# Projection of the queries in one step of 512 tokens and a short one, weight conversion without GpSimd, and a new order of all steps

## The chip, the cores and the metric

The kernel runs on one core of one Trainium2 chip. The metric is the device time of one launch in microseconds (us); three runs of the kernel before the change gave 1080.97, 1083.51 and 1084.04 us, with a median of 1083.51 us. One further execution was taken with the profiler: 1081.44 us, of which 1079.7 us lie between its first and its last instruction (the span). Five queues work side by side on the core: PE (TensorE, the matmuls), DVE (VectorE), ACT (ScalarE), POOL (GpSimd), and SP (SyncE), which here only issues DMAs. Each runs its own instructions strictly in the order in which they were written.

## What is computed

The reference is a linear attention with positive features, followed by a feed-forward layer whose activation is h cos(h). There are 8 batches of 8 heads, 576 tokens, a head size of 64, 128 features, a model width of 512 and a hidden width of 2048:

```python
def phi(x):
    proj = np.einsum('bhsd,df->bhsf', x, w_phi)
    proj = proj - np.max(np.abs(proj), axis=-1, keepdims=True)
    return np.concatenate([np.exp(proj), np.exp(-proj)], axis=-1)
q_p, k_p = (phi(q), phi(k))
kv = np.einsum('bhsf,bhsd->bhfd', k_p, v)
z = np.sum(k_p, axis=2)
num = np.einsum('bhsf,bhfd->bhsd', q_p, kv)
den = np.einsum('bhsf,bhf->bhs', q_p, z)[..., None] + 1e-06
attn = num / den                       # [8, 8, 576, 64]
x = attn.transpose(0, 2, 1, 3).reshape(4608, 512)
h = x @ w_in                           # [4608, 2048]
out = (h * np.cos(h)) @ w_out          # [4608, 512]
```

## The kernel before

**Units and visits.** Two heads form a pair, called a unit; there are 32 units (`attention(u)`). A unit's queries and keys lie with the 64 rows of one head on partitions 0 to 63 and those of the other on 64 to 127. The feed-forward layer works on chunks of 512 tokens; a `visit` takes one chunk through some or all of the 16 blocks of the hidden width. Each block needs one weight tile (a slice of both weight matrices).

**Feed-forward matmuls.** They are split in three products of a fast 32-bit format (high times high, high times low, low times high): `mm1` is 12 matmuls of 512 columns (line 782), `mm2` another 12 (lines 816 to 818). There are 144 of each in all.

**Weight tiles.** `convert(ft)` makes the high and low parts of a tile from the 64-bit inputs. ACT scales (lines 350, 351), DVE does three bit operations on 1024 columns (lines 355 to 359), ACT makes the high part, and three more elementwise instructions follow, `rest` (line 366), `low` (recorded as line 54) and `add` (line 372). `W_POOL` names the tiles for which POOL does these last three; it holds tiles 0 to 3. DVE does them for the other twelve. The first two visits need tiles 0 to 3, the third also 4 to 7, so these are converted while the first units run.

**Queries of a unit.** `q_mm(hf)` projects 288 tokens of both heads, one matmul for each head on its own half of the rows (line 434); it is called twice, as two steps. ACT copies the four results out of PSUM (`q_copy`, line 441), DVE reduces each to a maximum over blocks of 32 (`q_red`, line 445), then folds the maxima (lines 453, 454). POOL copies 32 partitions to the other three quarters (`q_spread`, line 459), DVE turns the maxima back into columns (`q_turn`, line 463), and POOL subtracts them from the projections (`q_sub`, line 467, two of 576 columns). ACT takes the exponentials (line 587).

**Keys of a unit.** `k_mm` projects 512 tokens of each head (line 476, eight small matmuls on half of the rows each) and `k_end` the last 64 of both heads in one full matmul (line 552). DVE takes the maxima (line 564). For the first eight units PE subtracts them in PSUM (`k_sub`, line 574), for the others DVE does (line 569).

**Shapes on PE.** Four shapes of the array are in use: all 128 x 128 (mm1, mm2, k_end, k_sub), rows in two halves (q_mm, k_mm), columns in two halves (lines 626, 632 and 675), and columns in four quarters (line 665). The 64-row pairs, the column pairs and the column quarters run side by side.

**What sets the order.** Every piece of work is a `Step` with an engine and an estimated cost. The table `ORDER` lists the numbers of all steps, 2920 of them, and the kernel issues them in that order; nothing is decided on the chip. A step's place in its engine's queue, and its PSUM bank, follow from the table. The steps touched by the change are those of `attention` for the queries and those of `convert` for tiles 0 to 3.

Of the kernel before, what the change touches and what calls it, by code (L numbers as in the profile page):

```python
# [17 lines left out]
P = 128  # L18
TWO_PI = 6.283185307179586
PI_2 = 1.5707963267948966  # L20
CT = 512
# [4 lines left out]
def phi_attention_then_cos_ffn(ctx: ExitStack, tc: tile.TileContext, qT, kT, vS, vT, w_phi, w_in, w_out, out):  # L26
# [41 lines left out]
    class Step:  # L68
# [16 lines left out]
    SHAPE = dict(mm1="full", mm2="full", one="full", k_mm="upper", k_end="full", t_mm="upper", t_end="full", s_mm="full", k_sub="full", kv_mm="left", n_mm="left", z_mm="quarter", q_mm="upper")  # L85
    ORDER = [
# [189 lines left out]
    def bank(b):  # L276
        return banks[b.slot]
# [26 lines left out]

    GROUP = 3
    Q_DVE = range(0)
    Q_SUMS = range(0)  # L310
    K_SUMS = range(8)
    WARM = 7
    WHOLE = 8
    W_POOL = range(4)
    Q = NFT // 4
    quarter = [list(range(Q * i, Q * i + Q)) for i in range(4)]
# [616 lines left out]
```

## Time and profile before

| what | value |
|---|---|
| median of three runs | 1083.51 us |
| the profiled execution, its own time | 1081.44 us |
| its span | 1079.7 us |
| mean granted TensorE clock | 1.000 |
| busy in the span: PE, ACT, DVE, POOL | 1069.3, 720.8, 711.8, 157.6 us |
| moved by DMA | 160.72 MB |

Busy time adds up every moment in which at least one instruction of an engine ran. For PE it says little by itself: matmuls overlap and their ends are modelled, so the interval from one start to the next is what counts. The prediction therefore reads PE's cost from starts in the timeline, and the cost of DVE, ACT and POOL from durations.

### The profile page before, as it was taken

The page shows a single profiled execution, that of the slowest core. Times are in us where ns is not written, and L with a number is a line of the kernel's source. Part 1 is how long each engine was busy: PE and PEld are TensorE (multiplying, and loading weights), DVE is VectorE, ACT ScalarE, POOL GpSimd, SP SyncE. Part 2 cuts the span into 40 slices and gives each one's busy share as a digit, 9 for nine tenths or more (in the row PEclk, how much of TensorE's full clock was granted, in tenths as well). Part 3 has the DMA queues.
Part 4 walks back from the last instruction along what each step waited for, and adds up shares of the span by engine and source line. Part 5 has one row for each costly group of instructions (what it writes and reads, how often), then busy time and mean ns, then how long its engine had stood idle before and what let it go on. Part 6 is the DMA issues. An engine that isn't in the chain of part 4 may idle for free.

```text
span 1079.7 us, 19604 instructions
## 1 busy us (share of the span) xinstructions
PE 1069.3 (99%) x7678; PEld 830.6 (77%) x7678; DVE 711.8 (66%) x1203; ACT 720.8 (67%) x1388; POOL 157.6 (15%) x187
## 2 busy tenths in 40 slices
PE   9999999999999999999999999999999999999998
PEld 6666677787888887788677787786877878888886
DVE  6899999988898877645667456764564353434333
ACT  7888898878666669754785766757556654544443
POOL 5664322000000310101121011120120000000000
PEclk9999999999999999999999999999999999999999
DMA  7535644667655544275242643163231720540541
GB/s 217 154 119 189 180 132 143 209 202 249 235 167 191 210 153 153 105 242 185 63 123 73 243 148 107 56 232 135 75 87 47 277 90 1 187 174 10 185 157 49
DMA packets 92604, 160.72 MB, mean 149 GB/s; under 512 B 43744, under 2 KB 52064, under 8 KB 84320
## 3 DMA queue, kind: packets, MB, share of 16 engines
q1 hardware_dynamic: 92352, 159.41, 44.3%
q8 instruction: 60, 0.98, 0.4%
q14 instruction: 32, 0.26, 0.1%
q10 hardware_dynamic: 160, 0.07, 0.0%
HBM read 117.51 MB, written 41.94 MB: 148 GB/s over the span
## 4 chain that ended last, share of the span: by engine, by line
PE 87%; DVE 5%; issue 0%; DMA 0%; POOL 0%; ACT 0%; DVEq 0%; POOLq 0%
PE bank L782 36%; PE bank L816 12%; PE bank L818 12%; PE bank L817 12%; PE bank L675 4%; PE bank L626 4%; PE bank L665 2%; PE bank L434 2%; PE bank L476 2%; PE bank L632 1%; PE bank L552 1%; DMA out<-o_last 0%; DVE g_c__1300 L793 0%; DVE g_c__1130 L800 0%; DVE m_u__1584 L445 0%
## 5 line engine op out<-in xcount | busy, mean ns | idle before, releaser
L797 ACT ACT_TABLE_LOAD x23 | 29.5, 1283 | 0.4
L459 POOL COPY m_u__4056<-m_u__4056 32x36 f32<-32x36 f32 x3 | 1.6, 540 | 174.4 <-DVE m_u__4056 L454 174.3
L582 ACT ACT_TABLE_LOAD x15 | 19.2, 1283 | 0.8 <-DVE pk_u__2466 L569 0.5
L856 DVE TENSOR_TENSOR o<-bank,o 128x512 f32<-128x512 f32 x24 | 16.1, 678 | 0.1
L863 ACT ACTIVATE o<-bank 128x512 f32<-128x512 f32 x16 | 9.5, 592 | 5.5 <-PE bank L818 5.5
L782 PE MATMUL bank<-xh_c__6319,w 128*128 128x512 f32 x32 | 12.9, 402 | 0.0
L865 DVE COPY o<-bank 128x512 f32<-128x512 f32 x16 | 10.8, 674 | 3.1 <-PE bank L818 3.1
L782 PE MATMUL bank<-xh_c__5560,w 128*128 128x512 f32 x32 | 12.7, 398 | 0.0
L782 PE MATMUL bank<-xh_c__7588,w 128*128 128x512 f32 x32 | 12.7, 396 | 0.0
L782 PE MATMUL bank<-xh_c__4428,w 128*128 128x512 f32 x32 | 12.6, 393 | 0.0
L782 PE MATMUL bank<-xh_c__6921,w 128*128 128x512 f32 x32 | 12.5, 391 | 0.0
L782 PE MATMUL bank<-xh_c__6769,w 128*128 128x512 f32 x32 | 12.5, 390 | 0.0
L782 PE MATMUL bank<-xh_c__5807,w 128*128 128x512 f32 x32 | 12.5, 390 | 0.0
L782 PE MATMUL bank<-xh_c__7130,w 128*128 128x512 f32 x32 | 12.5, 390 | 0.0
L782 PE MATMUL bank<-xh_c__5878,w 128*128 128x512 f32 x32 | 12.5, 390 | 0.0
L782 PE MATMUL bank<-xh_c__7977,w 128*128 128x512 f32 x32 | 12.5, 390 | 0.0
L782 PE MATMUL bank<-xh_c__5928,w 128*128 128x512 f32 x32 | 12.5, 390 | 0.0
L782 PE MATMUL bank<-xh_c__8059,w 128*128 128x512 f32 x32 | 12.5, 390 | 0.0
L782 PE MATMUL bank<-xh_c__4632,w 128*128 128x512 f32 x32 | 12.5, 389 | 0.0
L782 PE MATMUL bank<-xh_c__8100,w 128*128 128x512 f32 x32 | 12.5, 389 | 0.0
L782 PE MATMUL bank<-xh_c__4557,w 128*128 128x512 f32 x32 | 12.5, 389 | 0.0
L782 PE MATMUL bank<-xh_c__4759,w 128*128 128x512 f32 x32 | 12.4, 389 | 0.0
(3872 smaller groups left out, 4075.7 us busy)
## 6 DMA issues: line engine op xcount, KB each, us to landing
w<-w_parts SPq DMA_DIRECT2D x48, 1024.0 KB, 5.3
w_parts<-w SPq DMA_DIRECT2D x16, 1024.0 KB, 5.7
vmain<-vS SPq DMA_DIRECT2D x32, 256.0 KB, 3.9
out<-o SPq DMA_DIRECT2D x32, 256.0 KB, 3.5
sums<-o SPq DMA_DIRECT2D x24, 256.0 KB, 3.3
o<-sums SPq DMA_DIRECT2D x24, 256.0 KB, 3.2
vtail<-vT SPq DMA_DIRECT2D x64, 16.0 KB, 3.4
out<-o_last SPq DMA_DIRECT2D x4, 256.0 KB, 2.0
```

Of the source, the lines that this page charges most:

```text
L434: PE.matmul(out=ps[j], lhsT=wphi[r, :], rhs=d["qr"][r, hf * HALF:(hf + 1) * HALF], start=True, stop=True)
L476: PE.matmul(out=ps[j][:, P * s:P * s + P], lhsT=x[r, P * s:P * s + P], rhs=wphi[r, :], start=(s == 0), stop=w, skip_group_check=True)
L582: ACT.activation(out=e[:, :, s * P:(s + 1) * P], in_=pk, func=AF.Exp, scale=1.0 - 2.0 * s)
L626: PE.matmul(out=acc[c:c + 64, n, i, :], lhsT=e[:, s, P * n + c:P * n + c + 64], rhs=vmain[u % 2][:, s, i, :], start=(s == 0 and i == 0 and ...
L665: PE.matmul(out=ps[32 * g:32 * g + 32], lhsT=d["z"][:, 2 * n + j, :], rhs=d["eq", j][:, n, hf * HALF:(hf + 1) * HALF], start=(n == 0), sto ...
L675: PE.matmul(out=d["nps", hf][64 * j:64 * j + 64], lhsT=d["kv"][:, 2 * n + j, :], rhs=d["eq", j][:, n, cut[hf]], start=(n == 0 and hf == 0) ...
L782: PE.matmul(out=h, lhsT=a[:, cs], rhs=d[b, kt], start=(k == 0), stop=(k == 3 * KT - 1))
L797: ACT.activation(out=m["g"], in_=m["g"], func=AF.Sin, bias=halfpi, scale=1.0)
L816: PE.matmul(out=a, lhsT=gh[:, t], rhs=w[:, 0], start=first, stop=False)
L817: PE.matmul(out=a, lhsT=gh[:, t], rhs=w[:, 1], start=False, stop=False)
L818: PE.matmul(out=a, lhsT=gl[:, t], rhs=w[:, 0], start=False, stop=last)
L856: DVE.tensor_tensor(out=o, in0=bank(acc[tb]), in1=o, op=ALU.add)
```

## The change

The 576 query tokens of a head are no longer projected as two times 288 but as 512 and 64, as the keys already were: `q_mm` is one step of two matmuls with 512 columns, one for each head, and the new `q_end` is one full matmul of 128 columns for the last 64 tokens of both heads. ACT makes three copies instead of four, DVE two reductions of 576 columns instead of four of 288. The host lays out the queries accordingly, so the load of a unit's queries grows from 576 to 640 columns. `W_POOL` is empty: DVE does `rest`, `low` and `add` for all sixteen tiles. Code for another form of the query work that was not in use (`Q_SUMS`) is gone. The table `ORDER` is replaced as a whole and has 2824 numbers, 96 fewer, three for each unit.

```diff
     ORDER = [
-        0, 42, 17, 2, 5, 3, 4, 6, 7, 44, 47, 45, 49, 46, 48, 19, 21, 10, 8, 11, 9, 12, 20, 18, 22, 60, 23, 24, 59, 1,
...
+        2819, 2821, 2823,
     ]
...
-    W_POOL = range(4)
+    W_POOL = range(0)
...
-            d["qr"] = new("qr", [P, S + P], F32, f"qr_u{u}_")
+            d["qr"] = new("qr", [P, (NSLOT + 1) * P], F32, f"qr_u{u}_")
...
-            SP.dma_start(out=d["qr"][:, 0:S + P if u in Q_SUMS else S], in_=qT[u][:, 0:S + P if u in Q_SUMS else S])
+            SP.dma_start(out=d["qr"], in_=qT[u])
...
-        def q_mm(hf):
-            d["qps", hf] = ps = [bank(d["qb", hf, j])[:, 0:HALF] for j in range(2)]
+        def q_mm():
             for j in range(2):
                 r = slice(64 * j, 64 * j + 64)
-                PE.matmul(out=ps[j], lhsT=wphi[r, :], rhs=d["qr"][r, hf * HALF:(hf + 1) * HALF], start=True, stop=True)
+                PE.matmul(out=bank(qb[j]), lhsT=wphi[r, :], rhs=d["qr"][r, 0:CT], start=True, stop=True)
+
+        def q_end():
+            PE.matmul(out=bank(qb[2])[:, 0:P], lhsT=wphi, rhs=d["qr"][:, CT:CT + P], start=True, stop=True)
...
+            if i < 2:
+                ACT.activation(out=pq[:, i, 0:CT], in_=bank(qb[i]), func=AF.Copy, scale=1.0)
+            else:
+                ACT.activation(out=pq[:, :, CT:S], in_=bank(qb[2])[:, 0:P].rearrange("p (j s) -> p j s", j=2), func=AF.Copy,
+                               scale=1.0)
+
+        def q_red(j):
+            DVE.tensor_reduce(out=d["m1"][:, 2 * j * NJ:2 * (j + 1) * NJ],
+                              in_=d["pq"][:, j * S:(j + 1) * S].rearrange("p (j t) -> p j t", t=32), axis=AX.X,
                               op=ALU.max, apply_absolute_value=True, apply_transpose=True)
```

How the queues move is shown at three places. The first is PE, unit 21 in the middle of the program (names: `qr` the queries of a unit, `w` a weight tile, `gh` and `gl` the activations, `eq` and `kv`, `z` what a unit's queries and keys became). Before, one of its two query steps stands between a product of the feed-forward layer and the denominators of another unit:

```order
L817 MATMUL bank7_76<-w_5337,gh_c3__5530 128x512
L818 MATMUL bank7_76<-w_5337,gl_c3__5562 128x512
L434 MATMUL bank5_74<-qr_u21__5506,wphi_78 128x288
L434 MATMUL bank4_73<-qr_u21__5506,wphi_78 128x288
L665 MATMUL bank1_70<-eq_u19__5698,z_u19__5684 32x288
```

Now its short matmul stands between the numerators of another unit and the next product:

```order
L620 MATMUL bank1_70<-eq_u19__5598,kv_u19__5592 64x512
L620 MATMUL bank1_70<-eq_u19__5654,kv_u19__5592 64x512
L430 MATMUL bank5_74<-qr_u21__5103,wphi_78 128x128
L497 MATMUL bank7_76<-wphi_78,kr_u20__4795 128x128
L761 MATMUL bank2_71<-w_5358,gh_c3__5518 128x512
```

What moved: a unit has one step with the rows in two halves instead of two, and one with the full array, which shares its place with the short matmul of the keys (line 497, before line 552). Over the whole program the array changes its shape 153 times instead of 157, and it changes between the fast format and plain 32 bits within the full shape 69 times instead of 36.

The second place is DVE, where the maxima of the keys of units 6 and 7 (`mk`) are made for PE's subtractions. Before:

```order
L445 TENSOR_REDUCE m1_u5__826<-pq_u5__827 128x9
L564 TENSOR_REDUCE mk_u6__915<-bank6_75 128x1
L700 TENSOR_TENSOR rb_u3__912<-bank4_73,rb_u3__912 128x512
L564 TENSOR_REDUCE mk_u6__938<-bank7_76 128x4
L453 TENSOR_TENSOR m2_u5__941<-m1_u5__826 64x36
L454 TENSOR_TENSOR m3_u5__942<-m2_u5__941 32x36
L564 TENSOR_REDUCE mk_u6__945<-bank5_74 128x4
L564 TENSOR_REDUCE mk_u7__950<-bank1_70 128x1
```

Now:

```order
L509 TENSOR_REDUCE mk_u6__901<-bank4_73 128x4
L54 TENSOR_TENSOR xl3_c0__916<-rb_u3__894,xh3_c0__906 128x512
L360 TENSOR_TENSOR w_t2_f2__785<-w_t2_f2__785,w_t0_f2__783 128x1024
L509 TENSOR_REDUCE mk_u6__919<-bank6_75 128x1
L509 TENSOR_REDUCE mk_u7__921<-bank3_72 128x1
L54 TENSOR_TENSOR w_t1_f2__784<-w_t1_f2__784,w_822 128x1024
L444 TENSOR_REDUCE m1_u5__807<-pq_u5__808 128x18
L54 TENSOR_TENSOR xl2_c0__925<-rb_u2__706,xh2_c0__914 128x512
L452 TENSOR_TENSOR m2_u5__927<-m1_u5__807 64x36
L453 TENSOR_TENSOR m3_u5__928<-m2_u5__927 32x36
L366 TENSOR_TENSOR w_822<-w_t1_f2__784,w_t2_f2__785 128x1024
```

What moved: instructions of 1024 columns for tile 2 (`w_t2_f2`, `w_t1_f2`, `w_822`) stand between the maxima, and one of them stands between the fold of unit 5's maxima (`m3`) and its turn.

The third place is POOL in the first 50 us. Before:

```order
L459 COPY m_u__263<-m_u__263 32x36 x3
L366 TENSOR_TENSOR w_t_f__249<-w_t_f__249,w_t_f__247 128x1024
L467 TENSOR_TENSOR pq_u__157<-pq_u__157,bq_u__272 128x576 x2
L54 TENSOR_TENSOR w_t_f__248<-w_t_f__248,w 128x1024
L372 TENSOR_TENSOR w<-w_t_f__248,w_t_f__249 128x1024
L459 COPY m_u__480<-m_u__480 32x36 x3
```

Now:

```order
L458 COPY m_u__303<-m_u__303 32x36 x3
L466 TENSOR_TENSOR pq_u__173<-pq_u__173,bq_u__316 128x576 x2
L458 COPY m_u__449<-m_u__449 32x36 x3
L466 TENSOR_TENSOR pq_u__327<-pq_u__327,bq_u__507 128x576 x2
L458 COPY m_u__622<-m_u__622 32x36 x3
```

What moved: POOL has the copies and subtractions of the queries alone.

More of the change, by code (lines that the diff above doesn't have):

```diff
@@ L84, in phi_attention_then_cos_ffn @@
     SWITCH = dict(e=1.3, s=1.3, full=0.23, left=0.147, quarter=0.138, upper=0.195)
-    SHAPE = dict(mm1="full", mm2="full", one="full", k_mm="upper", k_end="full", t_mm="upper", t_end="full", s_mm="full", k_sub="full", kv_mm="left", n_mm="left", z_mm="quarter", q_mm="upper")
+    SHAPE = dict(mm1="full", mm2="full", one="full", k_mm="upper", k_end="full", q_end="full", k_sub="full", kv_mm="left", n_mm="left", z_mm="quarter", q_mm="upper")
     ORDER = [
[152 rows of a table removed]
[147 rows of a table added]
     ]
@@ L309, in phi_attention_then_cos_ffn @@
     Q_DVE = range(0)
-    Q_SUMS = range(0)
     K_SUMS = range(8)
@@ L477, in project @@
                               start=(s == 0), stop=w, skip_group_check=True)
-        def t_mm():
-            project([bank(qb[j]) for j in range(2)], d["qr"], True)
-        def t_end():
-            PE.matmul(out=bank(qb[2])[:, 0:P], lhsT=d["qr"][:, S:S + P], rhs=wphi, start=True, stop=True)
-        def t_max(i):
-            n = NSLOT if i < 2 else 1
-            if i == 0:
-                d["mq"] = new("pq", [P, 4 * NJ], F32, f"m1_u{u}_", "m1")
-            DVE.tensor_reduce(out=d["mq"][:, NSLOT * i:NSLOT * i + n],
-                              in_=bank(qb[i])[:, 0:P * n].rearrange("p (g f) -> p g f", f=P), axis=AX.X, op=ALU.max,
-                              apply_absolute_value=True)
@@ L493, in s_mm @@
-        def s_mm():
-            ps = [bank(sb_[i]) for i in range(3)]
-            for j in range(2):
-                r = slice(64 * j, 64 * j + 64)
-                PE.matmul(out=ps[j], lhsT=wphi[r, :], rhs=d["qr"][r, 0:CT], start=True, stop=False, skip_group_check=True)
-            PE.matmul(out=ps[2][:, 0:P], lhsT=wphi, rhs=d["qr"][:, S:S + P], start=True, stop=False, skip_group_check=True)
-            for i in range(3):
-                n = NSLOT if i < 2 else 1
-                for s in range(n):
-                    c = NSLOT * i + s
-                    PE.matmul(out=ps[i][:, P * s:P * s + P], lhsT=d["mq"][:, c:c + 1].broadcast_to([P, P]), rhs=minus,
-                              start=False, stop=True, skip_group_check=True)
@@ L506, in s_exp @@
-        def s_exp(j):
-            e = d["eq", j] = new("eq", [P, 2, S], F32, f"eq_u{u}_")
-            for s in range(2):
-                ACT.activation(out=e[:, s, 0:CT], in_=bank(sb_[j]), func=AF.Exp, scale=1.0 - 2.0 * s)
-            for s in range(2):
-                ACT.activation(out=e[:, s, CT:S], in_=bank(sb_[2])[:, 64 * j:64 * j + 64], func=AF.Exp, scale=1.0 - 2.0 * s)
-        eqs, eqb = [], []
-        if u in Q_SUMS:
-            qb = [Buf("bank", "a") for _ in range(3)]
-            sb_ = [Buf("bank", "a") for _ in range(3)]
-            tm = Step("PE", 0.88, t_mm, [ld], take=qb[:2] + [b["pq"]], use=[b["qr"]], kind="a.t_mm")
-            te = Step("PE", 0.22, t_end, [ld], take=qb[2:], use=[b["qr"]], kind="a.t_end")
-            tr = None
-            reds = []
-            for i in range(3):
-                tr = Step("DVE", 0.67 if i < 2 else 0.28, lambda i=i: t_max(i), [te if i == 2 else tm, tr], use=[qb[i], b["pq"]],
-                          kind="a.t_max")
-                reds.append(tr)
-            sm = Step("PE", 3.4, s_mm, reds, take=sb_, use=[b["qr"], b["pq"]], kind="a.s_mm")
-            qs = [sm]
-        else:
-            reds, mm = [], None
-            for hf in range(2):
-                pair = [Buf("bank", "a"), Buf("bank", "a")]
-                d["qb", hf, 0], d["qb", hf, 1] = pair
-                mm = Step("PE", 0.49, lambda hf=hf: q_mm(hf), [ld, mm], take=pair + ([] if hf else [b["pq"]]),
-                          use=[b["qr"]] + ([b["pq"]] if hf else []), kind=phase + "q_mm")
-                for j in range(2):
-                    cp = Step("ACT", 0.3, lambda hf=hf, j=j: q_copy(hf, j), [mm] + reds[:1], use=[pair[j], b["pq"]],
-                              kind=phase + "q_copy")
-                    reds.append(cp)
-            cps, reds = reds, []
-            for i, cp in enumerate(cps):
-                reds.append(Step("DVE", 0.37, lambda i=i: q_red(i // 2, i % 2), [cp], use=[b["pq"]], kind=phase + "q_red"))
-            qm = Step("DVE", 0.41, q_max, reds, take=[b["bq"]], use=[b["pq"]], port=True, kind=phase + "q_max")
-            qm = Step("POOL", 0.45, q_spread, [qm], use=[b["bq"]], port=True, kind=phase + "q_spread")
-            qm = Step("DVE", 1.3, q_turn, [qm], use=[b["bq"]], kind=phase + "q_turn")
-            qs = [Step(qname, qcost, lambda j=j: q_sub(j), [qm], use=[b["pq"], b["bq"]], port=True, kind=phase + "q_sub") for j in range(2)]
@@ new lines, in attention @@
+        eqs, eqb = [], []
+        qb = [Buf("bank", "a") for _ in range(3)]
+        mm = Step("PE", 0.86, q_mm, [ld], take=qb[:2] + [b["pq"]], use=[b["qr"]], kind=phase + "q_mm")
+        me = Step("PE", 0.14, q_end, [ld], take=qb[2:], use=[b["qr"]], kind=phase + "q_end")
+        cps = []
+        for i in range(3):
+            cps.append(Step("ACT", 0.52 if i < 2 else 0.2, lambda i=i: q_copy(i), [me if i == 2 else mm] + cps[:1], use=[qb[i], b["pq"]],
+                            kind=phase + "q_copy"))
@@ new lines, in attention @@
+        reds = [Step("DVE", 0.66, lambda j=j: q_red(j), [cps[j], cps[2]], use=[b["pq"]], kind=phase + "q_red")
+                for j in range(2)]
+        qm = Step("DVE", 0.41, q_max, reds, take=[b["bq"]], use=[b["pq"]], port=True, kind=phase + "q_max")
+        qm = Step("POOL", 0.45, q_spread, [qm], use=[b["bq"]], port=True, kind=phase + "q_spread")
+        qm = Step("DVE", 1.3, q_turn, [qm], use=[b["bq"]], kind=phase + "q_turn")
+        qs = [Step(qname, qcost, lambda j=j: q_sub(j), [qm], use=[b["pq"], b["bq"]], port=True, kind=phase + "q_sub") for j in range(2)]
@@ L601, in attention @@
                 kms[i] = Step("PE", 0.86 if i < 2 else 0.22, lambda i=i: k_sub(i), [kms[i]], use=[kb[i], pks[i]], kind="a.k_sub")
-        gate = [] if early or u in Q_SUMS or u in K_SUMS else kms + qs
+        gate = [] if early or u in K_SUMS else kms + qs
         eks, ekb = [], []
@@ L610, in attention @@
             e = Buf("eq")
-            eqs.append(Step("ACT", 1.15 if u not in Q_SUMS else 1.75, lambda j=j: (s_exp if u in Q_SUMS else exp_q)(j),
-                            ([sm] if u in Q_SUMS else [qs[j]]) + gate, take=[e], use=[sb_[j], sb_[2]] if u in Q_SUMS else [b["pq"]],
+            eqs.append(Step("ACT", 1.15, lambda j=j: exp_q(j),
+                            [qs[j]] + gate, take=[e], use=[b["pq"]],
                             table="e", kind=phase + "exp_q"))
@@ L898, in _arrange, with blocks @@
     m = S - n * P
-    def blocks(x, w):
+    def blocks(x):
+        w = n * P
         xp = x.reshape(NU, 2, S, D).transpose(0, 1, 3, 2)
@@ L908, in blocks @@
         return xT.reshape(NU, 2 * D, w + P)
-    qT, kT = blocks(q, S), blocks(k, n * P)
+    qT, kT = blocks(q), blocks(k)
     vp = v.reshape(NU, 2, S, D)
```

11 lines of the change are left out of this document (3 added, 8 removed), and 297 rows, old and new, of the table ORDER.

## The prediction

> **What bounds the kernel now.** The busy times and the chain of waits come first, then the stages, then what PE waits for.
>
> ```profile
> PE 1069.3 (99%) x7678; PEld 830.6 (77%) x7678; DVE 711.8 (66%) x1203; ACT 720.8 (67%) x1388; POOL 157.6 (15%) x187
> ...
> PE 87%; DVE 5%; issue 0%; DMA 0%; POOL 0%; ACT 0%; DVEq 0%; POOLq 0%
> ```
>
> PE has work for 99% of the span and makes up 87% of the chain that ends last. Nothing shortens this kernel that does not shorten PE's own queue or the moments in which PE waits. The view by stages (PE, weight loads, DVE, ACT, POOL) tells where these are:
>
> ```profile
> 0.00:54.00 54.00, 51.21 (x632) 34.76 (x636) 40.15 (x79) 43.22 (x101) 32.00 (x44) 1.00 0.62 186
> 54.00:135.00 81.00, 77.83 (x878) 51.98 (x872) 78.24 (x132) 69.54 (x152) 39.88 (x39) 1.00 0.52 163
> 135.00:216.00 81.00, 81.00 (x793) 60.99 (x790) 77.44 (x141) 73.66 (x150) 15.13 (x20) 1.00 0.50 162
> 216.00:1053.00 837.00, 837.00 (x5289) 664.79 (x5288) 506.80 (x840) 525.77 (x974) 70.60 (x85) 1.00 0.43 147
> ```
>
> After 135 us PE is never idle. Before, it is idle for 54 - 51.21 = 2.8 us and 81 - 77.83 = 3.2 us. In the second of these stages DVE is busy for 78.24 of 81 us, 97%: two engines are full at once there. The view of PE's waits names who lets PE wait:
>
> ```profile
> PE bank L887 <- DVE warm L289: 1.1, 1, 1.1
> ...
> PE bank L476 <- DMA kr_u__127<-kT: 0.8, 1, 0.8
> PE bank L574 <- DVE mk_u__915 L564: 0.8, 1, 0.8
> PE bank L574 <- DVE mk_u__945 L564: 0.8, 1, 0.8
> PE bank L574 <- DVE mk_u__938 L564: 0.7, 1, 0.7
> PE bank L434 <- DVE pk_u__1437 L569: 0.3, 1, 0.3
> ```
>
> Behind the start (1.1 + 0.8 = 1.9 us until the first data are there) it is DVE. So there are two questions: is PE's queue longer or shorter afterwards, and does DVE fall further behind in the first 135 us?
>
> **PE's queue: the queries.** The timeline of PE in a run of query steps, in the numerators of another unit, and around one short matmul of the keys (the second column is a modelled duration; I use the starts):
>
> ```profile
> 578.75 1.14 PE L434 MATMUL bank<-qr_u__5985,wphi 64*128 64x288 f32 x8
> 579.72 0.65 PE L434 MATMUL bank<-qr_u__5895,wphi 64*128 64x288 f32 x4
> ```
> ```profile
> 56.43 0.59 PE L675 MATMUL bank<-eq_u__702,kv_u__621 128*64 128x512 f32 x1
> ...
> 58.15 1.10 PE L626 MATMUL bank<-vmain,ek_u__782 128*64 128x65 f32 x32
> ```
> ```profile
> 581.56 0.39 PE L818 MATMUL bank<-w,gl_c__6272 128*128 128x512 f32 x1
> 581.80 0.38 PE L552 MATMUL bank<-wphi,kr_u__5896 128*128 128x128 f32 x2
> 581.93 0.48 PE L782 MATMUL bank<-xh_c__5560,w 128*128 128x512 f32 x1
> 582.25 0.40 PE L782 MATMUL bank<-xh_c__5878,w 128*128 128x512 f32 x1
> 582.48 0.40 PE L782 MATMUL bank<-xh_c__5807,w 128*128 128x512 f32 x1
> ```
>
> Each plain 32-bit matmul has two records, and two that share the array run side by side. Eight records of 288 columns, a unit's whole projection, take 579.72 - 578.75 = 0.97 us; call it 0.96, since they follow one another at 0.24. For 512 columns side by side there is the numerator: eight records in 58.15 - 56.43 = 1.72 us (0.1 of it for leaving that shape, below), so four, which is the new `q_mm`, take about 0.85; by columns it is 0.48 x 512 / 288 = 0.85 too. The new `q_end` has the form of `k_end`: from 581.56 to 582.25 lie 0.69 us for one fast matmul, `k_end` and another fast matmul; without it two fast ones take 2 x 0.23 (582.48 - 582.25) = 0.46, which leaves 0.23. Beside other plain 32-bit work it is nearer to 0.21. Sum per unit: 0.85 + 0.22 - 0.96 = +0.11 us, for 32 units **+3.5 us**.
>
> Changes of shape cost as well. A visit to the row halves between fast matmuls:
>
> ```profile
> 342.15 0.39 PE L782 MATMUL bank<-xl_c__3714,w 128*128 128x512 f32 x1
> 342.47 1.24 PE L434 MATMUL bank<-qr_u__3244,wphi 64*128 64x288 f32 x8
> 343.64 0.50 PE L782 MATMUL bank<-xh_c__3518,w 128*128 128x512 f32 x1
> 343.98 0.40 PE L782 MATMUL bank<-xh_c__3535,w 128*128 128x512 f32 x1
> ```
>
> The last fast matmul before takes 0.32 instead of 0.23, the visit 1.17 instead of 0.96, the first fast one after 0.34: 0.41 us for two changes, 0.2 for one. The new order has 153 changes instead of 157, and the entries into row halves, the dearest, fall from 47 to 41: about -4 x 0.2 = -0.8 us. The extra passages between fast and plain format are in the 0.23 above. **PE's queue grows by 3.5 - 0.7 = 2.8 us.** All of it lies on the path, because nothing else than PE sets the time after 135 us. This term I trust to about 1 us.
>
> **DVE in the first 135 us.** `rest` of a tile on both engines, then the reduction of 288 columns and the turn of 576 (the same number of columns as the new reduction):
>
> ```profile
> 0.00:216.00 216.00, 4.84 (x4) 9.52 (x4) 1.00 0.54 168
> ...
> 0.00:216.00 216.00, 24.53 (x60) 1.00 0.54 168
> ...
> 0.00:216.00 216.00, 10.55 (x14) 1.00 0.54 168
> ```
>
> Twelve instructions come to DVE at 4.84 / 4 = 1.21 us: +14.5 us. POOL gives up twelve at 9.52 / 4 = 2.38. Four reductions at 24.53 / 60 = 0.41 become two at 10.55 / 14 = 0.75: -0.13 us per unit, -1.0 for eight units.
>
> What comes back to DVE: some of its instructions take long while POOL converts. The timelines of POOL and of DVE:
>
> ```profile
> 44.79 2.37 POOL L54 TENSOR_TENSOR w_t_f__465<-w_t_f__465,w 128x1024 f32<-128x1024 f32 x1
> ...
> 63.55 2.34 POOL L54 TENSOR_TENSOR w_t_f__830<-w_t_f__830,w 128x1024 f32<-128x1024 f32 x1
> ...
> 77.60 2.41 POOL L366 TENSOR_TENSOR w_t_f__1049<-w_t_f__1049,w_t_f__1047 128x1024 f32<-128x1024 f32 x1 [4.14 <-ACT d_u__1080 L692]
> ```
> ```profile
> 45.69 2.02 DVE L54 TENSOR_TENSOR xl_c__743<-rb_u__640,xh_c__700 128x512 fp32r<-128x512 f32 x1 [1.01 <-ACT xh_c__700 L49]
> ...
> 64.61 1.33 DVE L453 TENSOR_TENSOR m_u__941<-m_u__826 64x36 f32<-64x36 f32 x1
> ...
> 67.01 0.67 DVE L54 TENSOR_TENSOR xl_c__1053<-rb_u__759,xh_c__888 128x512 fp32r<-128x512 f32 x1
> ...
> 77.49 0.19 DVE L453 TENSOR_TENSOR m_u__1099<-m_u__985 64x36 f32<-64x36 f32 x1
> 77.72 2.34 DVE L454 TENSOR_TENSOR m_u__1100<-m_u__1099 32x36 f32<-32x36 f32 x1
> ```
>
> 2.02 instead of 0.67, 1.33 instead of 0.19, 2.34 instead of about 0.19: 4.6 us of waiting for POOL that ends. I find no other of this size that coincides with a conversion. DVE also idles while POOL spreads the maxima, when nothing stands between the fold and the turn:
>
> ```profile
> 11.19 1.38 DVE L463 STREAM_TRANSPOSE bq_u__240<-m_u__171 128x1152 f32<-128x1152 f32 x1 [0.70 <-POOL m_u__171 L459]
> ...
> 30.71 1.38 DVE L463 STREAM_TRANSPOSE bq_u__486<-m_u__480 128x1152 f32<-128x1152 f32 x1 [0.87 <-POOL m_u__480 L459]
> ...
> 54.23 1.38 DVE L463 STREAM_TRANSPOSE bq_u__775<-m_u__769 128x1152 f32<-128x1152 f32 x1 [0.87 <-POOL m_u__769 L459]
> ...
> 96.29 1.38 DVE L463 STREAM_TRANSPOSE bq_u__1259<-m_u__1253 128x1152 f32<-128x1152 f32 x1 [0.87 <-POOL m_u__1253 L459]
> ```
>
> In the new order of DVE at least one longer instruction stands in this gap for each of the first nine units: -3.3 us. Sum: 14.5 - 1.0 - 4.6 - 3.3 = **+5.6 us of DVE's time** before the subtractions of unit 7's keys and the first visits are served. Queued behind these instructions on DVE are the maxima `mk` for which PE waits already.
>
> How much of it PE feels, no row tells, since the new order can put PE work that needs no DVE into the gap. The bounds: at best the 3.2 us of idle in the second stage vanish (-3.2); at worst all 5.6 show. The middle is +1.2; DVE at 97% of that stage pulls it towards the upper end, so I take **+2.0 us**.
>
> [...]
>
> **What costs nothing.** ACT makes one copy fewer per unit and has 81 - 69.54 = 11 us to spare in the second stage; without that cover the longer copies would cost a few tenths of a us at a unit's start. The query loads grow by 64 of 576 columns, 32 x 128 x 64 x 4 bytes = 1 MB in all, while the DMA engines are busy for half of each stage. SP issues the same number of transfers.
>
> **The sum.** 2.8 + 2.0 = +4.8 us. The profiled execution took 1081.44 us, which makes 1086.2; it lies 2.1 us under the median of 1083.51, from which it would be 1088.3. I predict **1087 us**.
>
> **Rivals.** *A wash*: the new order hides DVE's extra and takes about 3 us off PE's idle, as much as the queries cost: +0, 1081 to 1084 us. For it speaks that the gaps behind POOL are covered; against it that DVE's work ahead of PE grows.
>
> *Faster*: POOL's conversions hold up DVE for much longer than the three rows show, also where POOL's lateness makes ACT's exponentials and then PE late. They are 12 x 2.38 = 28.6 us of POOL; if more than 4.6 + 5.6 = 10.2 of them, a third, had cost DVE time, DVE gains on balance. Then PE's idle goes, 2.8 + 3.2 less the 1.9 of the start, and some 2 us of waits inside busy records: 2.8 - 4.1 - 2 = -3.3, 1078 to 1080 us. [...]
>
> *Much slower*: DVE becomes the bound of the whole first stage. All 5.6 us show on PE, and three or four of the new two-input instructions wait for a subtraction of POOL as others do now, about 2.38 x 576 / 1024 = 1.3 us each: 2.8 + 5.6 + 5 = +13, 1094 us. It decides from the point where the last of unit 7's maxima comes later than PE's other work lasts, around 90 us.
>
> **Chances.** The forecast (+3 to +8 us) 0.45, the wash 0.27, faster 0.13, much slower 0.15. A measurement of this kernel tells 0.3%, 3.25 us, from no change. The forecast holds some cases below that: slower 0.54, the same 0.32, faster 0.14. Two in ten may fall outside, so the range runs from 1079.5 to 1094; the forecast's own is 1084 to 1091.
>
> **What would show it.** PE's starts: eight records of a unit in about 0.85 us plus 0.22, and from 135 us to the end 2 to 3 us more than before for the same work. DVE at 95% or more up to 135 us, and PE's waits on `mk` summing to over 2.3 us. POOL without any 1024-column work, and no DVE instruction of 36 columns over 1.6 us. The prediction is wrong if PE's idle before 135 us falls under 3 us, or if the stretch after it is not longer.

## The result, and the profile after

The changed kernel takes **1087.49 us** (median of six runs, 1086.50 to 1089.94); the kernel before, run beside it, 1082.40 (six runs, 1080.74 to 1084.04). The ratio is 1.0053, 95% interval 1.0042 to 1.0065: slower by about 5 to 6 us. The forecast was 1087. The profiled execution took 1088.44 us, 7.0 more than that of the kernel before, with a span of 1086.7 us.

The busy times and the chain of waits of the changed kernel:

```profile
PE 1075.0 (99%) x7614; PEld 827.9 (76%) x7614; DVE 719.2 (66%) x1151; ACT 716.7 (66%) x1356; POOL 134.4 (12%) x175
...
PE 92%; DVE 6%; issue 1%; DMA 1%; ACT 0%; POOL 0%; ACTq 0%; DVEq 0%; POOLq 0%
```

Its stages (PE, weight loads, DVE, ACT, POOL, granted clock, DMA share, GB/s):

```profile
0.00:54.00 54.00, 49.84 (x558) 32.43 (x558) 42.61 (x67) 37.02 (x81) 17.87 (x35) 1.00 0.63 191
54.00:135.00 81.00, 77.91 (x823) 50.17 (x824) 78.01 (x127) 69.94 (x147) 30.66 (x34) 0.98 0.50 151
135.00:216.00 81.00, 81.00 (x865) 60.14 (x861) 76.31 (x130) 73.12 (x152) 18.53 (x22) 1.00 0.58 194
216.00:1053.00 837.00, 837.00 (x5251) 661.27 (x5251) 512.24 (x815) 525.53 (x960) 67.31 (x85) 1.00 0.43 146
```

PE is idle for 4.2 + 3.1 = 7.3 us before 135 us (6.0 before the change) and never from there to 1053 us. POOL gave up 157.6 - 134.4 = 23.2 us, DVE gained 719.2 - 711.8 = 7.4 us. In the second stage the granted clock is 0.98 instead of 1.00. PE's waits, the ones on the maxima of the keys (`mk`):

```profile
PE bank L519 <- DVE mk_u__1074 L509: 2.0, 1, 2.0
PE bank L519 <- DVE mk_u__670 L509: 1.9, 1, 1.9
...
PE bank L519 <- DVE mk_u__919 L509: 0.6, 1, 0.6
PE bank L519 <- DVE mk_u__901 L509: 0.5, 1, 0.5
```

They sum to 5.0 us. What is late in the longest of them shows in the timelines of POOL and of DVE:

```profile
78.27 4.06 POOL L466 TENSOR_TENSOR pq_u__808<-pq_u__808,bq_u__1045 128x576 f32<-128x576 f32 x2 [2.38 <-DVE bq_u__1045 L462]
```
```profile
78.04 0.65 DVE L349 TENSOR_SCALAR w_t_f__952<-w_t_f__952 128x1024 uint32<-128x1024 uint32 x1
78.73 2.31 DVE L351 SCALAR_TENSOR_TENSOR w_t_f__953<-w_raw_f__888,w_t_f__952 128x1024 uint32<-128x1024 uint32 x1
81.08 1.80 DVE L353 TENSOR_SCALAR w_t_f__952<-w_t_f__953 128x1024 uint32<-128x1024 uint32 x1
82.80 0.77 DVE L444 TRANSPOSE_TENSOR_REDUCE m_u__944<-pq_u__945 128x18 f32<-128x576 f32 x1
83.49 1.18 DVE L360 TENSOR_TENSOR w_t_f__954<-w_t_f__954,w_t_f__952 128x1024 f32<-128x1024 f32 x1
84.60 0.68 DVE L509 TENSOR_REDUCE mk_u__1074<-bank 128x4 f32<-128x512 f32 x1
```

While POOL subtracts a unit's maxima, two bit operations of tile 3, which DVE made before as well, take 2.31 and 1.80 us; undisturbed, line 351 takes 1.23 (tile 2) and line 353 0.69. That is 1.08 + 1.11 = 2.2 us. Behind them stands one of the twelve new instructions, and behind that the maxima for which PE waits. And PE, on its starts:

```profile
85.33 1.59 PE L519 MATMUL bank<-mk_u__1074,minus 128*128 128x512 f32 x2 [2.03 <-DVE mk_u__1074 L509]
85.93 1.42 PE L727 MATMUL bank<-xh_c__424,w 128*128 128x512 f32 x1
87.14 0.63 PE L727 MATMUL bank<-xh_c__662,w 128*128 128x512 f32 x1
87.57 0.63 PE L727 MATMUL bank<-xh_c__914,w 128*128 128x512 f32 x1
...
89.51 0.40 PE L727 MATMUL bank<-xh_c__906,w 128*128 128x512 f32 x1
89.75 0.39 PE L727 MATMUL bank<-xl_c__457,w 128*128 128x512 f32 x1
```

Behind the wait the fast matmuls follow one another at 87.57 - 87.14 = 0.43 us, later again at 0.24. The trace's record of the clock has it at one half from 85.85 to 89.27 us, 3.41 us. At 0.43 instead of 0.23 us for a fast matmul that costs about 3.41 x (0.43 - 0.23) / 0.43 = 1.6 us, an estimate. No term of the forecast had that.

### The profile page after: what moved, and what is told of

Same layout as the page of the kernel before. It is cut to its first block, busy times and chain, and to the rows that moved or that the text cites. A ratio compares the mean times of both kernels' runs of the same rounds, so it can differ in the third digit from the quotient of the medians.

```text
span 1086.7 us, 19383 instructions
## 1 busy us (share of the span) xinstructions
PE 1075.0 (99%) x7614; PEld 827.9 (76%) x7614; DVE 719.2 (66%) x1151; ACT 716.7 (66%) x1356; POOL 134.4 (12%) x175
## 4 chain that ended last, share of the span: by engine, by line
PE 92%; DVE 6%; issue 1%; DMA 1%; ACT 0%; POOL 0%; ACTq 0%; DVEq 0%; POOLq 0%
PE bank L727 36%; PE bank L761 12%; PE bank L762 12%; PE bank L763 12%; PE bank L620 5%; PE bank L571 4%; PE bank L610 3%; PE bank L427 3%; PE bank L473 2%; PE bank L577 1%; PE bank L430 1%; PE bank L497 1%; DMA wphi<-w_phi 0%; DVE w L366 0%; PE bank L519 0%
## 5 line engine op out<-in xcount | busy, mean ns | idle before, releaser
L727 PE MATMUL bank<-xh_c__6318,w 128*128 128x512 f32 x32 | 13.1, 410 | 0.0
L727 PE MATMUL bank<-xh_c__5380,w 128*128 128x512 f32 x32 | 13.0, 407 | 0.0
L727 PE MATMUL bank<-xh_c__7889,w 128*128 128x512 f32 x32 | 12.8, 402 | 0.0
L727 PE MATMUL bank<-xh_c__4376,w 128*128 128x512 f32 x32 | 12.5, 392 | 0.0
L727 PE MATMUL bank<-xh_c__5735,w 128*128 128x512 f32 x32 | 12.5, 391 | 0.0
L727 PE MATMUL bank<-xh_c__6704,w 128*128 128x512 f32 x32 | 12.5, 391 | 0.0
L727 PE MATMUL bank<-xh_c__5733,w 128*128 128x512 f32 x32 | 12.5, 391 | 0.0
L727 PE MATMUL bank<-xh_c__6524,w 128*128 128x512 f32 x32 | 12.5, 391 | 0.0
L727 PE MATMUL bank<-xh_c__8065,w 128*128 128x512 f32 x32 | 12.5, 391 | 0.0
L727 PE MATMUL bank<-xh_c__5856,w 128*128 128x512 f32 x32 | 12.5, 390 | 0.0
L727 PE MATMUL bank<-xh_c__7921,w 128*128 128x512 f32 x32 | 12.5, 390 | 0.0
L727 PE MATMUL bank<-xh_c__7010,w 128*128 128x512 f32 x32 | 12.5, 390 | 0.0
L727 PE MATMUL bank<-xh_c__8055,w 128*128 128x512 f32 x32 | 12.5, 390 | 0.0
L727 PE MATMUL bank<-xh_c__4531,w 128*128 128x512 f32 x32 | 12.5, 389 | 0.0
L727 PE MATMUL bank<-xh_c__4387,w 128*128 128x512 f32 x32 | 12.5, 389 | 0.0
L727 PE MATMUL bank<-xh_c__4677,w 128*128 128x512 f32 x32 | 12.4, 389 | 0.0
L727 PE MATMUL bank<-xh_c__8811,w 128*128 128x512 f32 x32 | 12.4, 389 | 0.0
```

The lines of the kernel that those rows point to most:

```text
L727: PE.matmul(out=h, lhsT=a[:, cs], rhs=d[b, kt], start=(k == 0), stop=(k == 3 * KT - 1))
```

## Experiments

All ratios are to the kernel before, run on the same chip in turns. My theory was the forecast's own: PE's queue grows by 2.8 us, and DVE's extra work is felt by PE through the waits on `mk`. The rivals: the queries are free and the order costs; POOL's conversions cost as much as DVE's; a wait that is taken away comes back.

### The queries alone

The old order with the new query steps, conversions on POOL. In `q_old_order` the second query step becomes the short matmul at its old place (on PE's queue):

```diff
-L434 MATMUL <-qr,wphi 128x288   (second q_mm, two matmuls)
+L430 MATMUL <-qr,wphi 128x128   (q_end, one matmul)
```

> The queries' part alone, put mechanically into the order of the kernel before: the second query step becomes the one matmul of the last 64 tokens, at the place where the second step stood; the conversions stay on POOL. My theory (PE's queue sets the time, priced by starts): the new matmul needs the full array and here often stands between steps with the rows in halves, so the array changes its shape 181 times instead of 157, and entries into row halves are 50 instead of 47. Priced with the intervals of the prediction (+0.11 us for each of 32 units, 0.2 us for each change of shape) PE's queue grows by 3.5 + 4.9 = 8.4 us: ratio to the kernel before 1.007 to 1.009. Rival 'the queries cost nothing, the rest of the new order does': 0.999 to 1.002. Rival 'changes of shape are hidden, only the work counts': 1.003.

In `q_old_order_placed` 21 of these short matmuls are moved on PE, next to other work on the full array.

> As the other kernel with the queries' part alone, but for 21 units the short query matmul stands elsewhere on PE, next to other work on the full array, so that there are 153 changes of shape, as in the changed kernel. By the same prices PE's queue is 3.0 us less 0.2 longer than in the kernel before, as in the changed kernel (2.8). My theory: 1.0025 to 1.0035, and 5.5 us less than the same change put mechanically. If the short matmul or its copy comes too late for DVE, up to 2 us more. Rival 'the queries cost nothing': 0.999 to 1.001. What then lies between this kernel and the changed one (1.0053) is what the conversions on DVE and the new order of the other steps cost: by my theory some 2 to 2.5 us.

Measured: 1091.45 us, ratio **1.0077** (1.0064 to 1.0090), for the mechanical form; that is +8.3 us, where the prices gave +8.4. In its trace PE also waits 1.6 us after 135 us (0.9 for a load of keys, 0.7 for `gl`), where the kernel before does not, and is idle for 1.4 us less before (4.6 instead of 6.0); the two nearly cancel. The moved form took 1090.15 us, **1.0066** (1.0054 to 1.0078), so of 5.5 us only 1.3 came. PE's waits of the moved form after 135 us:

```profile
PE bank L763 <- DVE gl_c__4800 L54: 1.1, 1, 1.1
PE bank L430 <- DMA qr_u__2026<-qT: 0.5, 1, 0.5
PE bank L427 <- DVE pk_u__1715 L514: 0.5, 1, 0.5
PE bank L610 <- ACT z_u__2081 L586: 0.3, 1, 0.3
```

They sum to 2.4 us (2.6 with one of 0.2 on a load of keys). 'The queries cost nothing' falls, and so does 'changes of shape are hidden'. My expectation for the moved form falls too. The places that are cheap for PE brought one short matmul ahead of its load (0.5 us) and one bank that came free late (0.5 us); the longest wait, on `gl`, is there in the mechanical form as well. The moved form took 7.1 us where the prices gave 2.8, and how the rest of these 4 us splits up I did not settle.

### The conversions alone

```diff
-    W_POOL = range(4)
+    W_POOL = range(0)
```

> The conversions' part alone: tiles 0 to 3 are converted by DVE, everything else as in the kernel before, in its order. My theory: DVE gets 14.5 us more and loses 4.6 us of waits for POOL, so some 10 us more, in an order that has no room for them; PE waits for the maxima in the first 135 us by 4 to 10 us more: ratio 1.004 to 1.009. Rival (the forecast's 'Faster': POOL's conversions held up DVE and ACT far more than three rows show): 0.997 to 1.001, with DVE less than 10 us busier.

And the reverse, the changed kernel with `W_POOL = range(4)`:

> The changed kernel with the conversions of tiles 0 to 3 back on POOL, in the new order, which was made without them. My theory: DVE is 14.5 us lighter before 135 us, PE's wait of 2.0 us for the maxima of unit 7 behind a conversion goes, and with it the drop of the granted clock; POOL's subtractions come later by up to 2.4 us each and DVE's two-input instructions meet POOL's: in all 1 to 3 us faster than the changed kernel, ratio to the kernel before 1.002 to 1.0045. Rival 'POOL's lateness in this order costs more than DVE's relief': 1.006 to 1.010.

Measured: 1090.17 us, **1.0070** (1.0058 to 1.0082) in the old order; 1086.13 us, **1.0032** (1.0021 to 1.0044) in the new order with POOL converting, against 1.0053 with DVE. The busy times, first of the conversions alone in the old order, then of the new order with POOL converting:

```profile
PE 1073.5 (99%) x7678; PEld 832.8 (77%) x7678; DVE 722.1 (66%) x1215; ACT 720.7 (66%) x1388; POOL 135.0 (12%) x175
```
```profile
PE 1072.5 (99%) x7614; PEld 826.6 (76%) x7614; DVE 714.8 (66%) x1139; ACT 716.9 (66%) x1356; POOL 159.1 (15%) x187
```

In the old order DVE gets 722.1 - 711.8 = 10.3 us: 14.5 of work less 4.2, which fits the waits of 4.6 us that the forecast saw ending. That this costs 7.6 us of time refutes the rival that POOL's conversions held DVE up much more. Halved clocks are part of it in most executions: four of the five have a mean granted clock of 0.994 to 0.998. In the new order the same conversions cost 719.2 - 714.8 = 4.4 us of DVE, since other instructions of DVE take longer there: lines 452, 738 and 54 have rows of 2.33, 2.24, 2.20 and 1.82 us that take 0.19, 0.65, 0.67 and 0.65 us in the changed kernel. That POOL's conversions hold them up is my reading of these rows. Of time the conversions cost 1.0053 - 1.0032, 2.3 us (0.5 to 4 by the intervals). So the price of an edit depends on the order around it: 7.6 us in the old one, about 2 in the one made for it.

### The two longest waits

DVE's queue in `maxima_u7_earlier`, against the changed kernel:

```diff
 L353 TENSOR_SCALAR w_t_f__952<-w_t_f__953 128x1024
+L509 TENSOR_REDUCE mk_u__1070<-bank_75 128x4
 L444 TENSOR_REDUCE m_u__944<-pq_u__945 128x18
 L360 TENSOR_TENSOR w_t_f__954<-w_t_f__954,w_t_f__952 128x1024
-L509 TENSOR_REDUCE mk_u__1074<-bank_75 128x4
```

> The changed kernel with one step moved on DVE: the maxima for the first keys of unit 7 (`mk`, for which PE waits 2.0 us at 83.3 us, the longest wait of the changed kernel) stand directly behind the bit operations of tile 3, ahead of a reduction of 0.77 us and of the new instruction of 1.18 us (`rest` of tile 3). Their input is there from 79.3 us. My theory: the wait shrinks from 2.0 to 0.3 us, and the granted clock is not halved for 3.4 us behind it, which costs 1.6 us: 1.7 to 3.3 us less than the changed kernel, ratio to the kernel before 1.0022 to 1.004. Rival 'DVE is simply overloaded up to 135 us, and a wait taken away here comes back at the next maxima': 1.005, within 0.5 us of the changed kernel.

`maxima_u7_u5_earlier` also moves the maxima `mk_u__670` and `mk_u__672` ahead of lines 626 to 630.

> As the kernel with the maxima of unit 7 moved, and besides the two maxima of unit 5 (PE waits 1.9 us for the first at 50 to 52 us) stand ahead of the three instructions for the inverse of unit 3's denominators (0.44 + 1.18 + 0.27 us). My theory: a further 1.5 to 1.9 us go, ratio 1.001 to 1.0025, unless the later inverse delays the first visits. Rival 'overloaded DVE': nothing, 1.005.

Measured: 1087.81 us, 1.0045 (1.0029 to 1.0060), which tells neither theory from the other; and 1086.32 us, 1.0031 (1.0019 to 1.0043). PE's waits between 40 and 60 us in the second one:

```profile
PE bank L519 <- DVE mk_u__677 L509: 1.7, 1, 1.7
```

The 1.9 us on unit 5's first maximum became 1.7 us on the next one of the batch (`mk_u__677`): the rival is right that the wait comes back. But that DVE is simply full is only half of it, as its timeline in the changed kernel shows:

```profile
49.93 1.18 DVE L628 TENSOR_SCALAR dn_u__651<-dn_u__651 128x9 f32<-128x9 f32 x1
```

This instruction has nine columns and takes 0.17 us elsewhere (at 76.4 us, for example). Here, and in the kernel with both moves, where it takes 1.33, it stands beside a subtraction of POOL (49.68 to 52.43 us in the changed kernel), and 1.0 to 1.2 us of either wait is its lateness.

What made this kernel faster is not settled. Its profiled execution has the full clock from 5.2 instead of 10.8 us (the start, see below), and the record of its eight executions has a mean granted clock of 1.000 in each, where five of the six of the changed kernel lie between 0.996 and 0.998: here no wait was followed by a halved clock. For unit 7 the executions differed at the start too, so the move was repeated with a start of its own.

### The start

```diff
-    WARM = 7
+    WARM = 9
```

> The changed kernel with nine instead of seven matmuls on zeros at the start (0.48 us each), so that PE has no gap of 0.7 us between them and the first data. In the profiled execution of the kernel before, the full clock was granted from 4.1 us, in that of the changed kernel from 10.8 us, and in four others between 9.0 and 9.7 us. Theory 'the clock's activity windows of 3.4 us': a window without a gap now ends before 8 us, so the full clock comes 1 to 3 us earlier, which is worth 0.5 to 1.5 us: ratio 1.004 to 1.005. Rival 'the start has nothing to do with the gap': 1.0053, the full clock at 9 to 11 us.

> The kernel before with nine instead of seven matmuls on zeros at the start. The times of the kernel before fall into two groups, about 1081.1 and about 1083.2 us. Theory 'the gap of 0.8 us before the first data decides whether an early window counts as busy': the full clock comes before 8 us in every execution, and the median falls from 1083 towards 1081.5 to 1082: ratio 0.998 to 0.9995. Rival 'the gap does nothing': 1.000 to 1.0003, the two matmuls more costing up to 0.3 us.

The windows of 3.4 us in the first theory are the 3.41 us of the clock's record (last section). That a window without a gap decides was the theory, which these two runs put to the test.

Measured: the changed kernel 1086.16 us, **1.0034** (1.0024 to 1.0045); the kernel before 1081.54 us, **0.9989** (0.9980 to 0.9997), eleven runs between 1080.87 and 1082.07, where with seven matmuls they lie between 1080.69 and 1085.06 (one run of 2165.96 us left out). PE's first rows, in the changed kernel with seven and in the kernel before with nine:

```profile
1.13 3.35 PE L832 MATMUL bank<-warm 128*128 128x128 f32 x14 [1.13 <-DVE warm L284]
5.22 0.77 PE L430 MATMUL bank<-qr_u__126,wphi 128*128 128x128 f32 x2 [0.73 <-DMA wphi<-w_phi]
5.92 2.08 PE L427 MATMUL bank<-qr_u__126,wphi 64*128 64x512 f32 x4
7.78 1.92 PE L473 MATMUL bank<-wphi,kr_u__127 64*128 64x128 f32 x16
```
```profile
1.13 4.21 PE L887 MATMUL bank<-warm 128*128 128x128 f32 x18 [1.13 <-DVE warm L289]
5.27 0.97 PE L476 MATMUL bank<-wphi,kr_u__129 64*128 64x128 f32 x9
```

With seven, PE has a gap of 0.7 us until the first data, and in this execution the four query matmuls then start 7.78 - 5.92 = 1.86 us before the next work instead of 0.96: the full clock came at 10.8 us. With nine there is no gap, and the clock's record has it full from 5.5 us in both kernels' profiles. By the ratios the gap cost the kernel before 1.2 us (0.3 to 2.2) and the changed one 2.1 us (0.4 to 3.7). It is there in both, and by these intervals the two costs can't be told apart. In the profiled executions they differ: with nine matmuls the changed kernel comes to the same matmul 2.3 us earlier (8.02 instead of 10.35 us), the kernel before only 0.3 us, since its profile with seven had the full clock from 4.1 us.

### Both together, and a kernel faster than both

> The changed kernel with nine matmuls on zeros at the start and with the maxima of unit 7 moved ahead of a reduction and of tile 3's `rest`. With seven matmuls at the start that move gave no difference that could be told, because its profiled execution lost time at the start and at 52 us by a halved clock. With a start that is always alike: theory 'the 2.0 us wait and the halved clock behind it cost 3 us' gives 1086.2 - 3.1 = 1083.1 us, ratio to the kernel before 1.0005 (1.000 to 1.0015). Rival 'overloaded DVE, the wait comes back at the next maxima': 1.003 to 1.004.

> The changed kernel with the conversions of tiles 0 to 3 back on POOL and nine matmuls on zeros at the start: what is left against the kernel before with nine is the queries and the new order of the other steps. My theory: PE's queue, 2.8 us, and no more of DVE than there: 1081.5 + 2.8 = 1084.3 us, ratio to the kernel before 1.0015 (1.0008 to 1.0022), and 1.9 us less than the changed kernel with nine. Rival 'the new order has waits of its own, whoever converts' (1.9 us at 50 us for the maxima of unit 5): 1.003 to 1.004.

> The kernel before with nine matmuls on zeros at the start, and on DVE the maxima of unit 6 (PE waits 0.8 + 0.7 + 0.8 us for three of them between 62.6 and 66.8 us) ahead of the turn and the products of unit 3 and of the fold of unit 5. A candidate that would be faster than both kernels. Theory 'only the order in which DVE serves counts': 1.5 to 2.3 us less than with nine matmuls alone, ratio 0.997 to 0.998. Rival 'DVE is full there, and what is put behind lets PE wait later': 0.9985 to 0.9995.

The last one moves, on DVE of the kernel before, three maxima of unit 6:

```diff
+L564 TENSOR_REDUCE mk_u__915
 L445 TENSOR_REDUCE m_u__826 (all four)
+L564 TENSOR_REDUCE mk_u__938
+L564 TENSOR_REDUCE mk_u__945
 L696 STREAM_TRANSPOSE rb_u__912
-L564 TENSOR_REDUCE mk_u__915
 L700 TENSOR_TENSOR rb_u__912 128x512
-L564 TENSOR_REDUCE mk_u__938
 L453 TENSOR_TENSOR m_u__941
 L454 TENSOR_TENSOR m_u__942
-L564 TENSOR_REDUCE mk_u__945
```

Measured: 1085.56 us, 1.0026 (1.0015 to 1.0036), for the changed kernel with both edits; 1084.64 us, **1.0020** (1.0011 to 1.0029), with POOL converting; 1080.23 us, **0.9980** (0.9971 to 0.9988), for the kernel before with both edits, the fastest kernel of this study.

- Queries and new order without DVE's conversions: 1.0020 - 0.9989 = 0.0031, 3.4 us (2.1 to 4.7 by the intervals). PE's 2.8 would fit, but it is not alone in there: the trace also has 0.7 us more of idle PE before 135 us (5.7 against 5.0 in the kernel before with nine) and a clock that is halved from 49.1 to 52.5 us, behind the wait of 1.9 us for unit 5's maxima.
- DVE's conversions in the new order: 1.0034 - 1.0020 = 0.0014, 1.5 us, no surer than its size (both intervals are 0.002 wide).
- The 2.0 us wait: taking it away gave 1.0034 - 1.0026 = 0.0008, 0.9 us (up to 2.5 by the intervals), not 3. PE's waits from 54 to 135 us in that kernel show a part of the reason:

```profile
PE bank L761 <- ACT z_u__1359 L586: 0.8, 1, 0.8
...
PE bank L519 <- DVE mk_u__1072 L509: 0.2, 1, 0.2
```

The wait for these maxima is 0.2 us, but 0.8 us for a copy by ACT, which the changed kernel did not have, came back 25 us later. A halved clock can still follow unit 5's wait: five of these ten executions have a mean granted clock of 0.997 or 0.998. And this profiled execution, 1087.21 us, had its full clock from 10.2 us only: the first weights came 0.6 us after the ninth matmul. So nine matmuls are not always enough in the changed kernel.

In the kernel before with both edits, PE's waits in that stretch are 1.6 us instead of 3.0:

```profile
PE bank L574 <- DVE mk_u__952 L564: 0.8, 1, 0.8
PE bank L574 <- DVE mk_u__937 L564: 0.3, 1, 0.3
PE bank L434 <- DVE pk_u__1439 L569: 0.3, 1, 0.3
PE bank L665 <- ACT eq_u__1250 L587: 0.2, 1, 0.2
```

The theory asked for 0.997 to 0.998 and got the upper end: one of the three waits moved to the next maximum. The interval also reaches into what the rival asked for (0.9985 to 0.9995), but PE's idle before 135 us fell from 5.0 to 3.6 us, and the median is 1.3 us under that with nine matmuls alone.

## Why the prediction was right, and where not

**PE's queue, +2.8 us: the prices right, the whole not shown.** (By the prediction's own terms it is 3.5 - 0.8 = 2.7.) The rows of the changed kernel carry the prices of the matmuls. One unit's query step, with the step after it, and two short matmuls between fast ones:

```profile
617.25 1.03 PE L427 MATMUL bank<-qr_u__6289,wphi 64*128 64x512 f32 x4
618.21 0.50 PE L761 MATMUL bank<-w,gh_c__6409 128*128 128x512 f32 x1
```
```profile
587.25 0.39 PE L727 MATMUL bank<-xl_c__5862,w 128*128 128x512 f32 x1
587.48 0.38 PE L430 MATMUL bank<-qr_u__5902,wphi 128*128 128x128 f32 x2
587.70 0.39 PE L430 MATMUL bank<-qr_u__5906,wphi 128*128 128x128 f32 x2
587.84 0.47 PE L727 MATMUL bank<-xh_c__5380,w 128*128 128x512 f32 x1
588.15 0.39 PE L727 MATMUL bank<-xh_c__5733,w 128*128 128x512 f32 x1
```

The step takes 618.21 - 617.25 = 0.96 us, of which 0.1 is for leaving the shape: 0.86, against 0.85. From 587.25 to 588.15 lie 0.90 us; less two fast matmuls (0.46) that is 0.22 for each short one, as forecast. Of three measurements two are near the prices, +8.3 us where they say 8.4 and 3.4 where they say 2.8, though both hold waits too. The third is not: the moved form took 7.1 us where they say 2.8.

The prediction also named a sign: 2 to 3 us more from 135 us to the end for the same work. It came out smaller. From 216 us on, both kernels have the queries of 17 units left, and PE never waits; the changed kernel takes 7.0 us more to its end, but has 27 fast matmuls more left to do (1572 + 1615 instead of 1560 + 1600), 6.2 us at 0.23. So the same work takes 0.8 us more. The prices themselves give 17 x 0.11 - 6 x 0.2 = 0.7 there, since 81 instead of 87 changes of shape lie in this stretch. The rest of the 2.8 would have to lie before 216 us, where PE also waits and the queue can't be read alone. An estimate from the two profiles with nine matmuls leaves less: they differ by 5.0 us, of which 0.5 is idle PE and up to 2 x 1.6 two halved stretches of the clock (49.9 to 53.3 and 84.1 to 87.5 us), so 1.3 or a little more remains for the whole queue. That the sum met the time so closely is then partly luck: the queue gave less, and the halved clock, which the forecast did not have, gave more.

**DVE's own time, +5.6 us: near in the sum, not in each term.** The busy times with the queries alone in the old order:

```profile
PE 1079.2 (99%) x7614; PEld 829.0 (76%) x7614; DVE 705.9 (65%) x1139; ACT 719.0 (66%) x1356; POOL 157.6 (14%) x187
```

The reductions gave more than thought: the row of `q_old_order` has 705.9 us of DVE, 5.9 less than before, where 32 times 0.13 is 4.2. The conversions in the old order gave the 14.5 less 4.2. Together these make +4.4; the changed kernel has +7.4. The 3 us between belong to the new order, and **"what comes back to DVE"** did not have them: the waits for POOL's conversions ended, and the idle before the turns (3.3 us) went, as forecast, but in the new order POOL's subtractions meet the bit operations (lines 349 to 353) of tiles 0 to 3. The groups of DVE up to 135 us, by form:

```profile
L351 DVE SCALAR_TENSOR_TENSOR w_t_f__489<-w_raw_f__461,w_t_f__488 128x1024 uint32<-128x1024 uint32 x1 | 2.3, 2331 | 0.0
L351 DVE SCALAR_TENSOR_TENSOR w_t_f__953<-w_raw_f__888,w_t_f__952 128x1024 uint32<-128x1024 uint32 x1 | 2.3, 2314 | 0.0
L351 DVE SCALAR_TENSOR_TENSOR w_t_f__224<-w_raw_f__166,w_t_f__223 128x1024 uint32<-128x1024 uint32 x1 | 2.3, 2308 | 0.0
L353 DVE TENSOR_SCALAR w_t_f__952<-w_t_f__953 128x1024 uint32<-128x1024 uint32 x1 | 1.8, 1800 | 0.0
L353 DVE TENSOR_SCALAR w_t_f__223<-w_t_f__224 128x1024 uint32<-128x1024 uint32 x1 | 1.8, 1781 | 0.0
L349 DVE TENSOR_SCALAR w_t_f__783<-w_t_f__783 128x1024 uint32<-128x1024 uint32 x1 | 1.7, 1667 | 0.0
L349 DVE TENSOR_SCALAR w_t_f__488<-w_t_f__488 128x1024 uint32<-128x1024 uint32 x1 | 1.5, 1523 | 0.0
```

Less 1.23 and 0.69 each, these are 7.3 us of waiting; before, one such row stood out (1.67). That is more than the 3 us; what ended elsewhere to make up for it was not added up row by row. Each of the seven started during one of POOL's subtractions (16.29 to 20.52, 39.34 to 42.57, 60.55 to 63.31 and 78.27 to 82.33 us). Lines 349 and 353 have a single input, and their rows took 1.52 to 1.80 instead of 0.69 us: not only instructions with two inputs were slow there. I had reckoned with such waits at the twelve new instructions only. These met no subtraction for long: the slowest took 1.49 us.

**"Felt by PE", +2.0 us: the right size, partly by luck.** Measured for the conversions alone: 2.3 us (1.5 with nine matmuls at the start), each with an interval of some 1.5 to 1.8 us either way. I had put it at the middle of -3.2 and +5.6 and raised it. In the old order the same edit cost 7.6 of the 10.3 us that DVE got, so most of DVE's time can be felt by PE: its later steps wait as well (`pk`, `rb`, a copy by ACT). And in the profiled execution 1.6 of the wait's 3.6 us was the halved clock, a mechanism that I did not have.

**Rivals.** *Faster* fell with the conversions alone (1.0070). *A wash* fell, since PE's idle grew from 6.0 to 7.3 us. *Much slower* had the right mechanism, a wait for POOL's subtraction, at the wrong instructions, and without its price. **What would show it**: the four records and the short matmul, PE's waits on `mk` (5.0 us), POOL without 1024 columns and DVE without long instructions of 36 columns came as said; the stretch after 135 us is longer, but by less than said (above). DVE's 95% holds for the second stage (78.01 of 81 us, 96%), not from the start (120.6 of 135 us, 89%).

## What to carry over

Price an engine's queue from the starts in the trace of before, changes of shape included: 8.4 us priced were 8.3 measured (6.9 to 9.7 by the interval) where the order was kept, but where steps were moved the same prices missed by 4 us. What an edit costs on a second engine that is nearly full can't be read from its own instructions: ask who stands behind them, and whether the new places let it wait for another engine, as DVE's bit operations did beside POOL's subtractions (2.31 instead of 1.23 us); the same twelve instructions cost 7.6 us in one order and about 2 in another. Before looking for the cause of the last 2 us, look at the start of the profiled executions: two profiles that differ by 7 us may differ by 5 in the kernel.

## What the runs showed of the hardware

The granted clock fell after 1.84 to 2.03 us of idle PE. The record of the clock has it at one half for 3.41 us at a time (85.85 to 89.27 us in the changed kernel), and the changes lie on a grid of 3.41 us (from 10.76 to 85.85 us there, 22 times 3.413); a window is one step of this grid. In the changed kernel the 3.41 us up to the drop at 85.85 hold 2.03 us of idle PE; in `maxima_u7_earlier` the two windows before drops hold 1.84 (start) and 1.94 us (at 52.1); with nine matmuls they hold 1.94 and 2.02 us in the changed kernel and 1.94 us with POOL converting. The wait of 1.95 us that ended at 52.01 in the changed kernel was followed by no drop: 1.66 us of it lay in one window, the rest in the next. In the kernel before, the most that one window holds behind the start is 1.52 us (62.1 to 65.5 us), and no drop followed. So in the windows measured here 1.84 us or more of idleness was followed by a halved clock and 1.66 us or less was not, and whether a 2 us wait cost a halved window depended on where it lay on the grid. For the first coming of the full clock these figures did not hold: it came only at 10.8 us in the changed kernel, with a gap of 0.73 us, and at 10.2 us in the one with both edits, with a gap of 0.57 us, while in `maxima_u7_u5_earlier` it came at 5.2 us although 0.7 us of a gap lay in the window before. No figure for it follows from these three. How often such drops come, the mean granted clock of every execution tells: one halved stretch takes 3.41 / 2 / 1085 = 0.0016 off it, the end of an execution, where PE is done, about 0.001 at most in these traces. It is 0.998 or less in five of six executions of the changed kernel and in five of eight with nine matmuls, but only in one of 61 of the kernel before that were run beside the experiments.
